# A spectral layer with a routed mixture of experts: first transfers reordered, expert tiles woven in pairs

## The chip, the cores and the metric

The kernel runs on one core of one Trainium2 chip. The metric is device time in microseconds, from the first to the last instruction of one execution; the number quoted for a kernel is the median of several executions. One further execution was taken with the hardware profiler, and all rows below are from it.

## What is computed

```python
X = np.fft.rfft(x, axis=1)                  # x is 8 x 2496 x 256, fp32
Yr = Xr @ w_r - Xi @ w_i + b_r              # 256 x 256 weights
Yi = Xr @ w_i + Xi @ w_r + b_i
Yr, Yi = shrink(Yr), shrink(Yi)             # sign(v) * max(|v| - 0.01, 0)
y = np.fft.irfft(Yr + 1j * Yi, n=2496, axis=1)
x = y.reshape(8 * 2496, 256)                # 19968 tokens
logits = x @ w_gate                         # 8 experts
e, g = argmax(logits), softmax(logits)[argmax]
out[token] = g * (max(x @ w1[e], 0) @ w2[e])   # w1 256 x 1024, w2 1024 x 256
```

## The kernel before

**Two stages.** The spectral stage computes the Fourier transforms as products with constant matrices and routes each token to a row of a DRAM table `xs` that is sorted by expert. The expert stage then walks over tiles of 256 rows of `xs`; a tile belongs to one expert.

**The spectral stage.** The length 2496 is split as 39 x 64. `fwd_a` (lines 274 to 287) multiplies pieces of x, loaded by `load_x` (lines 265 to 272, two DMAs per piece), with the constant `far` (or `fer` for the last piece), copies the result from PSUM to `ae` and stores it to a DRAM scratch `spec`. `turn` (lines 289 to 294) loads a transposed part of `spec` as the tile `t1` (`t` in the rows), two DMAs each. `fwd_b` (lines 296 to 304) multiplies it with the constant `bm`; `halves`, `mix` and `shrink` do the complex product with the weights (split into a rounded high part and a remainder, so that each product is three) and the threshold; `inv_b` and `inv_a` transform back with the constants `bi`, `ga` and `iw`. `iw` holds the gate's weights beside an identity, so that routing needs no product of its own. `route` (lines 554 to 629) computes each token's row in `xs` and leaves a list of eleven scatters in `self.rows`.

**Order of the work.** `spectral` (lines 402 to 504) writes the order out by hand for TensorE and SP (SyncE, which issues DMAs), and from line 442 on for ScalarE and VectorE too: 80 iterations, ten for each of eight batches. An iteration takes one pair of frequencies through `mix`, and holds the transforms of the next batch, the inverse of the last one and the loads four iterations ahead. Before the loop stand: `open_forward` (constants, x of batch 0, the weights, biases, and on POOL's queue nine loads of small constants), 18 warm-up matmuls on zeros, the eleven `fwd_a` of batch 0, `split_constants`, the first `turn`s with the rest of `bm` and the whole of `bi` between them, 17 more warm-up matmuls, and the first `fwd_b`. In iteration 3 the program calls `write_blank` (lines 222 to 232), eight DMAs on POOL's queue that write zero rows ahead of each expert's part of `xs`. Nothing ties them to that iteration.

**Marks.** `pace` (lines 550 to 552) lets POOL copy one element of a tile that was just written; scatters are tied behind the last such copy with a dependency on POOL's own order, and `send` issues one. So scatters are spread over the iterations. Marks are only made while there is something in `self.rows`.

**The expert stage.** There are 85 possible tiles. The last three (`RARE`) run only if a count that is known at run time, `live`, asks for them; 82 run with these inputs. The first five (`EARLY`) can start before the last routing is done. `load` (lines 733 to 750) loads a tile's rows: from tile 5 on as four DMAs for `xq` and one for `xr`. `upright` (lines 801 to 825) transposes them on VectorE (TensorE for the first five) and splits them into `xh` and `xl`. `weights` (lines 752 to 769) loads a tile's expert weights into `r1` and `r2`, two DMAs for w2 and eight for w1, skipped by the DMA itself when the expert is the same as the last tile's. `split1` and `split2` (lines 771 to 799) split them into high and low parts, each a ScalarE copy and a VectorE subtraction in four pieces, and then ask for the next tile's weights.

`step` (lines 896 to 898) does one tile: `up` (lines 827 to 854) makes the hidden layer as four PSUM tiles `ph` of two 128-column blocks, twelve matmuls of 256 columns each; ScalarE takes the Relu into `hh`, VectorE the remainder into `hl`. `down` (lines 856 to 894) makes the outputs in two halves of 128 rows: eight matmuls `hh` x [w2 high, w2 low] of 512 columns and eight `hl` x w2 high of 256 columns per half; then ScalarE and VectorE scale by the gate value (`part`, `o`) and POOL scatters 128 rows of the output. `up` of a tile carries `upright` of the next, `down` carries `split2` and `split1` of the next. `experts_rest` (lines 917 to 941) loops over tiles 3 to 81, then reads `live` on every engine and has three conditionals one after the other.

Of the kernel before, what the change touches and what calls it, by code (L numbers as in the profile page):

```python
# [10 lines left out]
F32 = mybir.dt.float32  # L11
F32R = mybir.dt.float32r
# [12 lines left out]
D = 256  # L25
# [73 lines left out]
class Kernel:  # L99
# [80 lines left out]
    def open_forward(self, st):  # L180
        tc, nc, nb = self.tc, self.nc, self.nb
        f = self.f = self.pool(st, "f", 1, side="right")
        self.xp = self.pool(st, "xp", 5, side="right")
# [10 lines left out]
        self.bias = f.tile([128, 2, D], F32, name="bias")  # L194
        self.bias3 = f.tile([128, 2 * D], BF16, name="bias3")
        nc.vector.memset(self.bias3, 0.0)
        self.xg = {}
# [3 lines left out]
        raw = {}  # L201
# [4 lines left out]
        self.raw = raw  # L206
        for h, b in ((0, self.b_r), (1, self.b_i)):
            nc.gpsimd.dma_start(self.bias[:, h, :], b.rearrange("(o n) -> o n", o=1).broadcast_to((128, D)))
        self.nlam = f.tile([128, 1], F32, name="nlam")
        nc.vector.memset(self.nlam, -LAM)  # L210

        nc.gpsimd.dma_start(self.gar, self.c_ga)
        for c in range(2):
            nc.gpsimd.dma_start(self.iw[:, c, c * 128:c * 128 + 8], self.w_gate[c * 128:(c + 1) * 128, :])
        nc.gpsimd.dma_start(self.ids, self.c_ids)
        nc.gpsimd.dma_start(self.score, self.c_score)
        nc.gpsimd.dma_start(self.base, self.c_base)
        nc.gpsimd.dma_start(self.ltri_f, self.c_ltri)
        nc.gpsimd.dma_start(self.tcol, self.c_tcol)
        nc.gpsimd.memset(self.z[:, :, 64:66, :], 0.0)  # L220

    def write_blank(self):
# [4 lines left out]
        for e in range(E):  # L227
            i = nc.gpsimd.dma_start(self.xs[e * self.cap:e * self.cap + TT, :].rearrange("(p h) c -> p h c", h=2),
                                    blank)
            if e:  # L230
                tc.declare_no_dep(i.ins, group="xs", reason="disjoint rows")
            tc.add_to_no_dep_group("xs", i.ins)

    def split_constants(self):
        nc, f, raw = self.nc, self.f, self.raw
        ws = self.w.tile([128, 2, D], F32, tag="r", name="wsum")
        wd = self.w.tile([128, 2, D], F32, tag="r", name="wdif")
        nc.vector.tensor_sub(wd, raw["i"], raw["r"])
        nc.vector.scalar_tensor_tensor(out=ws, in0=raw["i"], scalar=-1.0, in1=raw["r"], op0=ALU.mult, op1=ALU.subtract)
        raw = {"r": raw["r"], "d": wd, "s": ws}  # L240
        for nm in ("s", "d", "r"):
            self.wh[nm] = f.tile([128, 2, D], F32R, name="wh" + nm)
            self.wl[nm] = f.tile([128, 2, D], F32R, name="wl" + nm)
            nc.scalar.copy(self.wh[nm], raw[nm])
            nc.vector.tensor_sub(self.wl[nm], raw[nm], self.wh[nm])
        self.split_bias()
        nc.scalar.copy(self.gh, self.gar)
        nc.vector.tensor_sub(self.gl, self.gar, self.gh)
        for c in range(2):
            nc.vector.tensor_copy(self.iw[:, c, 8 - 8 * c:136 - 8 * c], self.ident)  # L250
        nc.vector.tensor_copy(self.ltri, self.ltri_f)


# [11 lines left out]
    def load_x(self, b, q):  # L265
        n, j = (4, 3) if q < 5 else (2, 2)
        t = self.xp.tile([117, 4, D], F32, tag="x", name="x")
        for lo, hi in ((0, 32), (32, NA)):
            src = bass.AP(self.x.tensor, self.x[b, NB * lo + 4 * q, 0].offset,
                          [[NB * D, hi - lo], [22 * D, j], [1, n * D]])  # L270
            self.nc.sync.dma_start(t[lo * j:hi * j, :n, :].rearrange("p g d -> p (g d)"), src)
        self.xg[b, q] = t

    def fwd_a(self, b, q, g):
# [5 lines left out]
        ae = self.xp.tile([120, 2, D], F32, tag="ae", name="ae", bufs=8)  # L280
# [121 lines left out]
    def spectral(self, fwd):  # L402
# [563 lines left out]
```

## Time and profile before

| what | us |
|---|---|
| median of 3 runs | 1580.95 |
| lowest, highest | 1579.96, 1581.32 |
| the profiled execution's own time | 1581.68 |
| its span (first to last instruction) | 1579.8 |
| mean granted TensorE clock in it | 0.988 |

How the rows are read: times are us from the start of the span, unless marked ns. PE is TensorE's matmuls and PEld its weight loads, DVE is VectorE, ACT ScalarE, POOL GpSimd, and a q behind an engine's name is its issuing queue (SPq issues DMAs). L841 is line 841 of the kernel. `out<-in` names tiles, `xN` is a count, and what stands in brackets is the idle time of the engine just before and what ended it. A busy time of a group of matmuls counts from its first start to its last modelled end; single matmuls overlap, so the distance between starts is the better measure of pace. PEclk is the granted clock, 1.00 for 2.4 GHz and 0.50 for 1.2 GHz.

### The profile page before, as it was taken

Reading aid. Unit: us, or ns where it says so; the run is one execution under the profiler, and the core shown is the slowest. Engines: PE = TensorE matmul, PEld = TensorE weight load, DVE = VectorE, ACT = ScalarE, POOL = GpSimd, SP = SyncE. Lnnn points to the kernel's source line nnn. Section 1 sums busy time; section 2 is a strip of 40 time slices with the busy share of each in tenths; the row PEclk is TensorE's granted clock in tenths of the full one; section 3 lists DMA queues with packets and bytes.
Section 4 is the critical chain, followed back from the end, with each engine's and each line's share of the span. In section 5 each row is a group of like instructions: output and inputs, shape, how many; then the busy total and the mean of one; then the engine's idle time right before and its main releaser. Section 6 shows DMA issues by size and latency. Waiting matters only on the chain. (4 is left out here: it accounts for less than half of the span.)

```text
span 1579.8 us, 35881 instructions
## 1 busy us (share of the span) xinstructions
PE 1524.4 (96%) x10881; PEld 1398.3 (89%) x10883; DVE 1248.8 (79%) x2685; ACT 1078.5 (68%) x2255; POOL 542.1 (34%) x529
## 2 busy tenths in 40 slices
PE   5999999999999898999999999999999999999996
PEld 2789988988989888889999999999999999999996
DVE  3577776778787987878888888888888888888886
ACT  1577776767677667567676767676767677776765
POOL 2000624244251634723333233334343333333333
PEclk8899999999999999999999999999999999999998
DMA  8753645445462314243223224223214123223120
GB/s 262 214 164 92 192 114 165 139 143 165 130 185 81 120 33 137 83 103 98 51 45 98 49 49 98 48 48 98 49 45 100 45 52 92 55 68 75 42 49 20
DMA packets 182931, 153.81 MB, mean 97 GB/s; under 512 B 120378, under 2 KB 154080, under 8 KB 182477
## 3 DMA queue, kind: packets, MB, share of 16 engines
q1 hardware_dynamic: 162829, 107.17, 26.7%
q0 software_dynamic: 19904, 44.29, 8.5%
q8 instruction: 88, 1.44, 0.4%
q14 instruction: 110, 0.90, 0.2%
HBM read 243.33 MB, written 66.37 MB: 196 GB/s over the span
## 5 line engine op out<-in xcount | busy, mean ns | idle before, releaser
L889 POOL DMA_INDIRECT out<-o,row x154 | 303.7, 1972 | 573.7 <-DVE o L887 548.7
L879 PE MATMUL po<-h,hh 128*128 128x512 f32 x1312 | 462.1, 396 | 0.0
L841 PE MATMUL ph<-xh,h 128*128 128x256 f32 x1312 | 372.8, 284 | 4.0 <-DVE hl L847 2.3
L841 PE MATMUL ph<-xh,l 128*128 128x256 f32 x1312 | 372.1, 284 | 0.5 <-DVE l L782 0.3
L841 PE MATMUL ph<-xl,h 128*128 128x256 f32 x1312 | 371.8, 283 | 0.0
L846 ACT ACTIVATE hh<-ph 128x512 fp32r<-128x512 f32 x328 | 196.0, 597 | 241.0 <-PE ph L841 241.0
L847 DVE SCALAR_TENSOR_TENSOR hl<-ph,hh 128x512 fp32r<-128x512 f32 x328 | 226.7, 691 | 141.0 <-ACT hh L846 130.7
L876 PE MATMUL po<-h,hl 128*128 128x256 f32 x1148 | 321.9, 280 | 0.4 <-DVE hl L847 0.4
L879 PEld LDWEIGHTS po<-h,hh 128*128 128x128 f32 x1312 | 241.4, 188 | 44.4 <-issue 0.2
L841 PEld LDWEIGHTS ph<-xh,h 128*128 128x128 f32 x1312 | 251.9, 192 | 5.0 <-DVE hl L847 3.1
L841 PEld LDWEIGHTS ph<-xh,l 128*128 128x128 f32 x1312 | 252.1, 192 | 4.5 <-DVE l L782 1.0
L841 PEld LDWEIGHTS ph<-xl,h 128*128 128x128 f32 x1312 | 252.0, 192 | 0.0
L876 PEld LDWEIGHTS po<-h,hl 128*128 128x128 f32 x1148 | 217.0, 189 | 4.5 <-DVE hl L847 0.7
L782 DVE TENSOR_TENSOR l<-r,h 128x512 fp32r<-128x512 f32 x332 | 207.1, 686 | 4.4 <-ACT h L781 4.4
L797 DVE TENSOR_TENSOR h<-r,h 128x512 fp32r<-128x512 f32 x332 | 207.1, 685 | 1.2 <-ACT h L796 1.1
L620 POOL DMA_INDIRECT xs_dram<-yb,pos x176 | 180.6, 1026 | 75.5 <-issue 38.1
L781 ACT CAST h<-r 128x512 fp32r<-128x512 f32 x332 | 180.6, 618 | 3.0 <-DMA r<-moe_w 3.0
L796 ACT CAST h<-r 128x512 fp32r<-128x512 f32 x332 | 180.5, 618 | 0.8 <-DMA r<-moe_w 0.8
L358 DVE SCALAR_TENSOR_TENSOR y<-v,r 64x256 f32<-64x256 f32 x320 | 133.9, 418 | 6.8 <-ACT r L352 1.6
L315 DVE TENSOR_TENSOR su<-re,pb 128x256 f32<-128x256 f32 x80 | 33.6, 420 | 91.8 <-ACT sh L314 61.9
L302 PE MATMUL pb<-bm,t 128*128 128x128 f32 x640 | 86.3, 279 | 15.3 <-DMA t<-spec_dram 13.2
L552 POOL COPY mark<-v 1x1 f32<-1x1 f32 x52 | 9.4, 180 | 261.3 <-DVE v L344 261.0
(180 smaller groups left out, 2856.9 us busy)
## 6 DMA issues: line engine op xcount, KB each, us to landing
r<-moe_w SPq DMA_DIRECT2D x178, 512.0 KB
r<-moe_w SPq DMA_DIRECT2D x632, 128.0 KB
spec_dram<-ae SPq DMA_DIRECT2D x88, 240.0 KB
t<-spec_dram SPq DMA_DIRECT2D x160, 128.0 KB
xq<-xs_dram SPq DMA_DIRECT2D x312, 64.0 KB
x<-x SPq DMA_DIRECT2D x40, 384.0 KB
x<-x SPq DMA_DIRECT2D x40, 84.0 KB
xs_dram<-yb,pos POOLq DMA_INDIRECT x176, 3.2
```

The lines of the kernel that those rows point to most:

```text
L358: nc.vector.scalar_tensor_tensor(out=y[q * 64:q * 64 + 64, kp, :], in0=u[h, q, :], scalar=LAM, in1=r[h, q, :], op0=ALU.add, op1=ALU.min)
L620: i = nc.gpsimd.indirect_dma_start(out=self.xs[:, :], out_offset=bass.IndirectOffsetOnAxis(ap=pos[:n, g:g + 1], axis=0), in_=y[:n, g, 0:XW ...
L781: nc.scalar.copy(hi[:, c, s], v)
L782: nc.vector.tensor_sub(lo[:, c, s], v, hi[:, c, s])
L796: nc.scalar.copy(hi[:, s, :], v)
L797: nc.vector.tensor_sub(lo[:, s, :], v, hi[:, s, :])
L841: nc.tensor.matmul(p[:, i, :], a[:, c, f * 128:(f + 1) * 128], v[:, c, :], start=m == 0, stop=m == 5)
L846: nc.scalar.activation(hh[:, s, :], p, AF.Relu)
L847: nc.vector.scalar_tensor_tensor(out=hl[:, s, :], in0=p, scalar=0.0, in1=hh[:, s, :], op0=ALU.max, op1=ALU.subtract)
L876: nc.tensor.matmul(p[:, :D], hl[:, f - 1, hs], w2[:, f - 1, 0, :], start=False, stop=False)
L879: nc.tensor.matmul(p, hh[:, f, hs], w2[:, f].rearrange("p a d -> p (a d)"), start=f == 0, stop=f == 7)
L889: i = nc.gpsimd.indirect_dma_start(out=self.out[:, :], out_offset=bass.IndirectOffsetOnAxis(ap=at[h], axis=0), in_=o[:, h, :], in_offset=N ...
```

## The change

What it does, in the order of the program:

- `open_forward`: `fer`, the smaller DMA of each x piece of batch 0 and later the order on SP change: SP issues `far` and the larger x pieces, ScalarE's queue the smaller ones and `fer`. One more buffer for x, eleven instead of eight for `ae`. The biases come as three rows each (six DMAs of 1 KB on POOL's queue, into a tile that VectorE zeroes) instead of two broadcasts to 128 partitions, and are split ahead of the transforms.
- `load_weights`, then blocks 0 to 3 of `bm`, stand on SP behind the stores of `ae`, right ahead of the first `turn`. The rest of `bm` and all of `bi` go in pieces of four blocks (128 x 512 fp32), in front of the loop and in iterations 0 to 6.
- The nine small constants go on SP's queue in iterations 7 and 8 (`load_late`), and what is computed from them follows in iterations 9 and 10 (`late_constants`).
- `write_blank` becomes a generator in `self.rows`, so each of the eight blocks is issued behind a mark, from iteration 3 on.
- 24 instead of 17 warm-up matmuls ahead of the first `fwd_b`.
- Experts: from tile 3 on, `up(3)` runs alone, then `pair(t)` weaves `down` of tile t with `up` of tile t + 1, four parts of four slots, each slot three matmuls of up and two of down. It carries `split2(t + 1)`, `split1(t + 2)` and `upright(t + 2)`. `hh` and `hl` have a second buffer (pool `hb`) for even tiles. Rows are loaded five tiles ahead instead of four. The last `down(81)` runs alone.
- Nothing is prepared any more for a tile that may not run; `live` is read behind the first `pair`, and the three rare tiles become nested conditionals that load and split their own weights.

```diff
 def open_forward(self, st):
...
-        self.xp = self.pool(st, "xp", 5, side="right")
+        self.xp = self.pool(st, "xp", 6, side="right")
...
         nc.sync.dma_start(far, self.c_fa)
-        nc.sync.dma_start(self.fer, self.c_fe)
...
         for q in range(6):
-            self.load_x(0, q)
-        nc.sync.dma_start(self.bm[:, 0:4, :], self.c_bm[:, 0:4, :])
...
+            self.load_x(0, q, nc.scalar)
+            if q == 1:
+                nc.scalar.dma_start(self.fer, self.c_fe)
+                self.load_bias()
...
+    def load_bias(self):
+        self.bias = self.w.tile([128, 2, D], F32, tag="bias", name="bias", bufs=1)
+        self.nc.vector.memset(self.bias, 0.0)
+        for row in (0, 32, 64):
+            for h, b in ((0, self.b_r), (1, self.b_i)):
+                self.nc.gpsimd.dma_start(self.bias[row:row + 1, h, :], b.rearrange("(o n) -> o n", o=1))
...
+    def load_late(self, part):
+        nc = self.nc
+        if part == 0:
+            nc.sync.dma_start(self.gar, self.c_ga)
+            for c in range(2):
+                nc.sync.dma_start(self.iw[:, c, c * 128:c * 128 + 8], self.w_gate[c * 128:(c + 1) * 128, :])
+            nc.sync.dma_start(self.ltri_f, self.c_ltri)
+        else:
+            nc.sync.dma_start(self.ids, self.c_ids)
+            nc.sync.dma_start(self.score, self.c_score)
+            nc.sync.dma_start(self.base, self.c_base)
+            nc.sync.dma_start(self.tcol, self.c_tcol)
...
 def write_blank(self):
...
-            if e:
-                tc.declare_no_dep(i.ins, group="xs", reason="disjoint rows")
-            tc.add_to_no_dep_group("xs", i.ins)
+            self.behind_mark(i, e > 0)
+            yield
...
 def spectral(self, fwd):
...
         self.keep_warm(18)
+        self.split_bias()
         for i in pairs:
             self.fwd_a(0, *i)
+        self.load_weights()
+        self.blocks(self.bm, self.c_bm, 0, 4)
+        self.turn(0, 0)
         self.split_constants()
-        self.turn(0, 0)
         self.turn(0, 1)
-        self.nc.sync.dma_start(self.bm[:, 4:, :], self.c_bm[:, 4:, :])
+        self.blocks(self.bm, self.c_bm, 4, 8)
         self.turn(0, 2)
         if nb > 1:
             self.load_x(1, 0)
-        self.nc.sync.dma_start(self.bi, self.c_bi)
         self.turn(0, 3)
...
-        self.keep_warm(17)
+        self.keep_warm(24)
...
-            if it == 3:
-                self.write_blank()
+            for at, to, src, lo in ((0, self.bm, self.c_bm, 8), (0, self.bi, self.c_bi, 0),
+                                    (1, self.bm, self.c_bm, 12), (2, self.bi, self.c_bi, 4),
+                                    (3, self.bm, self.c_bm, 16), (4, self.bi, self.c_bi, 8),
+                                    (5, self.bi, self.c_bi, 12), (6, self.bi, self.c_bi, 16)):
+                if at == it:
+                    self.blocks(to, src, lo, lo + 4)
+            if it in (7, 8):
+                self.load_late(it - 7)
...
+            if it == 3:
+                self.rows.append(self.write_blank())
...
+    def pair(self, t):
+        nc = self.nc
+        xh, xl = self.xts.pop(t + 1)
+        h1, l1 = self.ws.pop((t + 1, 1))
+        hh, hl = self.hs.pop(t)
+        w2 = self.ws.pop((t, 2))
+        self.room(t + 1)
+        done = self.outputs(t)
+        splits = itertools.chain(self.split2(t + 1), self.split1(t + 2))
+        turn = self.upright(t + 2)
+        for part in range(4):
+            h, hs = part // 2, slice(part // 2 * 128, part // 2 * 128 + 128)
+            if part % 2 == 0:
+                po = self.psb.tile([128, 512], F32, tag="o", name="po")
+            ph = (self.psb if part % 2 else self.psa).tile([128, 2, TT], F32, tag="h", name="ph")
+            for j in range(4):
+                i, c = j // 2, j % 2
+                f = part * 2 + i
+                for m, (a, v) in enumerate(((h1, xh), (l1, xh), (h1, xl))):
+                    nc.tensor.matmul(ph[:, i, :], a[:, c, f * 128:(f + 1) * 128], v[:, c, :],
+                                     start=c == 0 and m == 0, stop=c == 1 and m == 2)
+                f = part % 2 * 4 + j
+                for g in (f - 1, f) if f == 7 else (f - 1,) if f else ():
+                    nc.tensor.matmul(po[:, :D], hl[:, g, hs], w2[:, g, 0, :], start=False, stop=False)
+                nc.tensor.matmul(po, hh[:, f, hs], w2[:, f].rearrange("p a d -> p (a d)"), start=f == 0, stop=f == 7)
+            next(splits, None)
+            next(turn, None)
+            next(splits, None)
+            self.hidden(t + 1, part, ph)
+            if part % 2:
+                done(h, po)
+        for _ in itertools.chain(splits, turn):
+            pass
...
 def experts_rest(self, late):
...
-        for t in range(t0, main):
-            if t + 4 <= main:
-                self.load(t + 4)
-            self.step(t)
-        live = self.nc.values_load(self.tabs[1][0:1, 3, 0:1], min_val=0, max_val=self.nt)
-        nt = self.nt
-        for t in range(main, nt):
-            with self.tc.If(live > t - self.early):
-                if t > main:
-                    self.nt = t
-                    self.weights_now(t)
-                self.nt = t + 1
-                self.up(t)
-                self.down(t)
+        lead = itertools.chain(self.upright(t0 + 1), self.split1(t0 + 1))
+        self.up(t0, lead)
+        for _ in lead:
+            pass
+        for t in range(t0, main - 1):
+            self.load(t + 5)
+            self.pair(t)
+            if t == t0:
+                live = self.nc.values_load(self.tabs[1][0:1, 3, 0:1], min_val=0, max_val=last)
+        self.down(main - 1)
+        self.rare(live, main, last)
+
+    def rare(self, live, t, last):
+        if t == last:
+            return
+        with self.tc.If(live > t - self.early):
+            self.weights_now(t)
+            self.up(t)
+            self.down(t)
+            self.rare(live, t + 1, last)
```

## Rows read from the trace of the kernel before

**Rows 1.** The page's head and one of its groups of instructions (busy, mean).

```profile
span 1579.8 us, 35881 instructions
...
L879 PE MATMUL po<-h,hh 128*128 128x512 f32 x1312 | 462.1, 396 | 0.0
```

**Rows 2.** Busy time of each engine in chosen stretches, with clock and transfers.

```profile
core 0: us, PE busy (x) PEld busy (x) DVE busy (x) ACT busy (x) POOL busy (x), PEclk, DMA share, GB/s
0.00:36.10 36.10, 21.00 (x57) 7.67 (x58) 11.44 (x32) 6.72 (x11) 11.57 (x27) 0.93 0.83 256
50.40:53.40 3.00, 0.22 (x3) 0.05 (x2) 0.81 (x2) 0.00 (x0) 0.00 (x0) 1.00 0.59 150
53.40:60.90 7.50, 7.50 (x39) 6.12 (x40) 2.94 (x7) 4.22 (x9) 0.00 (x0) 0.77 0.88 250
60.90:83.50 22.60, 22.60 (x157) 18.70 (x156) 14.52 (x32) 15.56 (x35) 0.00 (x0) 1.00 0.62 185
687.09:698.48 11.39, 9.25 (x49) 8.56 (x49) 5.46 (x9) 4.33 (x8) 1.59 (x2) 0.70 0.29 63
704.10:1567.46 863.36, 863.36 (x6081) 808.92 (x6079) 733.77 (x1293) 610.33 (x1141) 299.71 (x153) 1.00 0.26 63
```

**Rows 3.** TensorE in order of time, first 37 us (start us, us, instruction).

```profile
1.40 6.75 PE L509 MATMUL pw<-idle 128*128 128x512 bf16 x18 [1.40 <-DVE idle L155]
...
20.93 1.02 PE L278 MATMUL pa<-x,fer 78*120 78x512 f32 x2
...
36.07 2.05 PE L302 MATMUL pb<-bm,t 128*128 128x128 f32 x8 [10.45 <-DMA t<-spec_dram]
```

**Rows 4.** TensorE in order of time, one tile of the steady expert stage.

```profile
1181.22 0.28 PE L841 MATMUL ph<-xh,h 128*128 128x256 f32 x1
...
1182.28 0.28 PE L841 MATMUL ph<-xh,h 128*128 128x256 f32 x1
...
1186.96 0.40 PE L879 MATMUL po<-h,hh 128*128 128x512 f32 x1
...
1190.14 0.40 PE L879 MATMUL po<-h,hh 128*128 128x512 f32 x1
...
1192.58 0.28 PE L841 MATMUL ph<-xh,h 128*128 128x256 f32 x1
```

**Rows 5.** All engines in order of time, the last instructions of the span.

```profile
1567.22 0.40 PE L879 MATMUL po<-h,hh 128*128 128x512 f32 x1
...
1568.55 0.48 DVE L887 SCALAR_TENSOR_TENSOR o<-po,xr,part 128x256 f32<-128x256 f32 x1
1569.80 0.98 POOL L889 DMA_INDIRECT out<-o,row  x1 [0.30 <-DVEq L935]
```

**Rows 6.** DMA issues by line (count, KB of each, us to landing).

```profile
xs_dram<-blank POOLq DMA_DIRECT2D x8, 264.0 KB, 7.6
...
bi<-c_bi SPq DMA_DIRECT2D x1, 1280.0 KB
...
bias<-b_r POOLq DMA_DIRECT2D x1, 128.0 KB
```

**Rows 7.** SP's queue in order of time, first 61 us (start, us, DMA).

```profile
1.62 10.27 SPq L271 DMA_DIRECT2D x<-x  x12
...
16.48 12.37 SPq L287 DMA_DIRECT2D spec_dram<-ae  x11
32.59 2.60 SPq L293 DMA_DIRECT2D t<-spec_dram  x4
```

**Rows 8.** SP's queue in order of time, 663 to 705 us.

```profile
667.35 1.99 SPq L746 DMA_DIRECT2D xq<-xs_dram  x4
...
678.14 7.39 SPq L769 DMA_DIRECT2D r<-moe_w  x10
```

**Rows 9.** ScalarE in order of time, 685 to 700 us.

```profile
689.18 1.66 ACT L781 CAST h<-r 128x512 fp32r<-128x512 f32 x3 [2.26 <-DMA r<-moe_w]
```

**Rows 10.** Waits, 704 to 1560 us (us in total, times, longest).

```profile
DVE hl L847 <- ACT hh L846: 118.8, 226, 0.8
```

More of the change, by code (lines that the diff above doesn't have):

```diff
@@ L270, in load_x @@
                           [[NB * D, hi - lo], [22 * D, j], [1, n * D]])
-            self.nc.sync.dma_start(t[lo * j:hi * j, :n, :].rearrange("p g d -> p (g d)"), src)
+            (other if other and lo else self.nc.sync).dma_start(t[lo * j:hi * j, :n, :].rearrange("p g d -> p (g d)"), src)
         self.xg[b, q] = t
@@ L622, in scatter @@
                     in_=y[:n, g, 0:XW], in_offset=None, bounds_check=E * self.cap - 1, oob_is_err=False)
-                tc.declare_no_dep(i.ins, group="xs", reason="disjoint rows")
-                tc.add_to_no_dep_group("xs", i.ins)
-                tc.add_manual_dep(i.ins, self.paced.ins.name, mybir.DependencyInfo(
-                    mybir.DependencyClass.NoSync, mybir.DependencyReason.DATA), reason="a few rows per slot")
+                self.behind_mark(i)
                 yield
@@ L831, in up @@
         h1, l1 = self.ws.pop((t, 1))
[L832 to L833 removed]
+        self.room(t)
         for f2 in range(4):
@@ L868, in down, with done @@
         o = self.w2p.tile([128, 2, D], F32, tag="o", name="o", bufs=2)
+        def done(h, p):
+            part = self.w2p.tile([128, D], F32, tag="part", name="part", bufs=2)
+            nc.scalar.activation(part, p[:, D:], AF.Copy, scale=xr[:, h, 0:1])
+            nc.vector.scalar_tensor_tensor(out=o[:, h, :], in0=p[:, :D], scalar=xr[:, h, 0:1], in1=part,
+                                           op0=ALU.mult, op1=ALU.add)
+            i = nc.gpsimd.indirect_dma_start(
+                out=self.out[:, :], out_offset=bass.IndirectOffsetOnAxis(ap=at[h], axis=0),
+                in_=o[:, h, :], in_offset=None, bounds_check=self.ntok - 1, oob_is_err=False)
+            if t or h:
+                tc.declare_no_dep(i.ins, group="out", reason="every token is in one tile only")
+            tc.add_to_no_dep_group("out", i.ins)
+        return done
+    def down(self, t):
+        nc = self.nc
+        hh, hl = self.hs.pop(t)
+        w2 = self.ws.pop((t, 2))
+        done = self.outputs(t)
         work = (self.split2(t + 1), self.split1(t + 1))
@@ L884, in down @@
                 self.send(2)
-            part = self.w2p.tile([128, D], F32, tag="part", name="part", bufs=2)
-            nc.scalar.activation(part, p[:, D:], AF.Copy, scale=xr[:, h, 0:1])
-            nc.vector.scalar_tensor_tensor(out=o[:, h, :], in0=p[:, :D], scalar=xr[:, h, 0:1], in1=part,
-                                           op0=ALU.mult, op1=ALU.add)
-            i = nc.gpsimd.indirect_dma_start(
-                out=self.out[:, :], out_offset=bass.IndirectOffsetOnAxis(ap=at[h], axis=0),
-                in_=o[:, h, :], in_offset=None, bounds_check=self.ntok - 1, oob_is_err=False)
-            if t or h:
-                tc.declare_no_dep(i.ins, group="out", reason="every token is in one tile only")
-            tc.add_to_no_dep_group("out", i.ins)
+            done(h, p)
     def step(self, t):
@@ L898, in step, with room, hidden @@
         self.down(t)
+    def room(self, t):
+        pool = self.hb if self.hb and t % 2 == 0 else self.w2p
+        self.hs[t] = [pool.tile([128, 8, TT], F32R, tag=n, name=n) for n in ("hh", "hl")]
+    def hidden(self, t, f2, p):
+        nc = self.nc
+        hh, hl = self.hs[t]
+        s = slice(f2 * 2, f2 * 2 + 2)
+        nc.scalar.activation(hh[:, s, :], p, AF.Relu)
+        nc.vector.scalar_tensor_tensor(out=hl[:, s, :], in0=p, scalar=0.0, in1=hh[:, s, :],
+                                       op0=ALU.max, op1=ALU.subtract)
+    def pair(self, t):
+        nc = self.nc
+        xh, xl = self.xts.pop(t + 1)
+        h1, l1 = self.ws.pop((t + 1, 1))
+        hh, hl = self.hs.pop(t)
+        w2 = self.ws.pop((t, 2))
+        self.room(t + 1)
+        done = self.outputs(t)
+        splits = itertools.chain(self.split2(t + 1), self.split1(t + 2))
[23 more added lines that the diff above has]
+            pass
     def experts_begin(self):
```

90 lines of the change are left out of this document (45 added, 45 removed).

## The prediction

> **What bounds the kernel now.** I read the span first, then the table by stretches, then the transfers and the engines' order of time inside the stretches that stood out. The span is 1579.8 us [rows 1]. From 704.10 to 1567.46 us TensorE is busy for the whole 863.36 us at a granted clock of 1.00, while VectorE works 733.77 us of it (85%) and ScalarE 610.33 us (71%) [rows 2]. That stretch holds 6081 matmuls; a tile has 80 (48 up, 32 down), so it is 76 tiles of 11.36 us. No engine is waited for by TensorE there, so work saved on VectorE or ScalarE, or a wait taken away, is worth nothing in it. Only a closer spacing of the matmuls would be.
>
> What isn't full is the start. In the first 36.1 us TensorE's real work is the column transforms, done by about 22 us; then it idles 10.45 us for `t<-spec_dram` [rows 3], and that window moves 256 GB/s [rows 2], which says that transfers set its end. Later TensorE is nearly idle from 50.4 to 53.4 us (0.22 us busy), and the next 7.5 us run at a mean clock of 0.77: part of it is at 1.2 GHz instead of 2.4 after that pause [rows 2]. Two more places lose time: tile 5, where up takes 11.39 us instead of 5.74 at a mean clock of 0.70 [rows 2, 4], and the end, where the last matmul starts at 1567.22 us, 12.6 us before the span's end [rows 1, 5].
>
> **The start.** The first inverse-order product needs, in a chain, x, the copies `ae`, their stores, and the loads `t`. Moved away from in front of it are eight zero blocks of 264 KB (2.16 MB), two biases of 128 KB (0.26 MB) that become six rows of 1 KB, and nine loads of small constants (about 0.29 MB by their shapes) [rows 6]: together 2.7 MB. The window moved 36.1 x 256 = 9.24 MB, so 6.5 MB are left; at the same 256 GB/s this takes 25.5 us instead of 36.1, a gain of 10.6 us. The other bound is the chain itself: TensorE can't start before its warm-up ends at 8.15 us; if x is through by 14 us instead of 20.93 [rows 3] (its 2.5 MB at 256 GB/s take 10 us, behind some 3 us of start), a copy (about 1 us), a store's landing (last stores end their issue near 28.85, the loads of `t` go out at 32.59: 3.7 us [rows 7]) and the first load (36.07 - 32.59 = 3.5 us) end at 22.5 us, a gain of 13.6 us. I take 12.
>
> Putting x on two queues is worth the issue alone: SP issues twelve pieces in 10.27 us, until 11.89 [rows 7], but x keeps coming until 20.93 [rows 3], so transfers, not the issue, set it. I cost it at nothing by itself; ScalarE's seven issues at some 0.86 us each (10.27 / 12) end near 8 us, before the first transform gives it a copy to do. The weights behind the stores take about 0.5 MB out of x's way and still land before the first mix; their splits (ScalarE and VectorE, 0.6 to 0.7 us each) run while `t` is loaded. Eleven instead of eight `ae` buffers take away a wait of the last three copies on landed stores; this lies inside the 12. `bm` in pieces and `bi` in pieces behind the first iteration leave 0.26 MB each ahead of the loads of `t`, where the rest of `bm` and the whole of `bi` (1.31 MB [rows 6]) stand now: the 2.8 us of idle go, and so does most of the 1.2 GHz stretch after it (0.23 x 7.5 = 1.7 us, since 0.5 would be half): I take 4 us together. What is late next: the blocks, the pieces of `bi` and nine constants now move during iterations 0 to 8, some 4 MB. At 60.9 to 83.5 us the queues were busy 0.62 with 185 GB/s [rows 2], so 0.38 x 22.6 us x 300 GB/s = 2.6 MB are free in such a stretch and the rest spreads; the loads of `t` are asked for four iterations ahead. POOL did nothing in that stretch (0.00 us), so the eight blocks behind marks block nobody there. I give back 1 us. Start: -15 us; ends -8 (only the later stall and part of the bytes) and -18.
>
> **The expert tiles.** `pair` runs down of tile t and up of tile t+1 woven: three up products of 256 columns, then one 256-column and one 512-column product of down, sixteen times. The count of products and columns is unchanged, so what counts is spacing. In the steady tile the first nine up products take 1181.22 to 1182.28 = 0.118 us each, the other 39 take 0.120, and the pairs of down 3.18 / 9 = 0.353 us up to 1190.14 and 2.44 / 7 = 0.349 behind it [rows 4]. So after a run of 512-column products the next nine are closer by 2 ns, as if TensorE lived for a while on weights loaded ahead. Woven, every fifth product has 512 columns. Nearest row for up: the 0.118 behind a down; for down the mean (5.62 / 16 = 0.351). Per slot 3 x 0.118 + 0.351 = 0.705, per tile 11.28, that is 0.08 to 0.1 us less; times 76: -7 us. Ends: all at the closest spacing (3 x 0.116, a third of 0.349, + 0.349, 11.15) -16 us, all at the widest (3 x 0.120 + 0.353, 11.41) +4 us; a spacing that the trace does not show at all may lie beyond, so I let the far end go to +14.
>
> [...]
>
> VectorE's and ScalarE's work per tile stays. SP loads x five tiles ahead instead of four; the weights of the next expert are asked for behind the same splits. The splits for tile 82, which is not computed (1312 products of each kind are 82 tiles of 16 [rows 1]), lie beside matmuls; their end saves only what stands in the last chain.
>
> **Around tile 5** the change costs something. Its loads wait for the last scatters (667.35), SP then issues loads and ten weight pieces until 685.5 [rows 8], and ScalarE gets the last of the weights at 689.18 [rows 9]. Now up of tile 5 stands ahead of down of tile 4, so half a tile (5.6 us) of work that used to fill this wait comes behind it. Against that, w1's pieces now go out ahead of the two of w2, 2 x 0.74 us sooner (7.39 / 10). 5.6 - 1.5 = 4.1; some of it falls into the 1.2 GHz stretch that today follows the wait, so I take +3 us, ends 0 and +7.
>
> **The end.** Behind the last matmul stand a copy, the product `o` at 1568.55, the read of the tile count and the last scatter at 1569.80, and three conditionals [rows 5]. The count is now read long before and the skipped conditionals are one. Of the 9 us after 1570.78 the landing stays; I take -2 us, ends 0 and -4.
>
> **Sum.** -15 - 7 + 3 - 2 = -21 us. The profiled execution took 1581.68 us in all, 0.73 above the median of the three runs, 1580.95; from the median it comes to 1560 us.
>
> **The rivals.** (A) Order doesn't matter to TensorE: -14 us, 1567. For it: inside up there is no wait whatever; against it: 0.118 and 0.120 for the same products in one tile. (B) The start is held by x and its stores whatever else moves, and only the later stall goes: -4 instead of -15, 1571. For it: the queues were busy 0.83 in the first window; against it: 2.6 MB of that is not x. (C) All products at the closest spacing or below: -31 or more, 1550 down. (D) The other side: VectorE becomes the bound of a pair. It is in order, each `hl` stands behind ScalarE's `hh`, and in the steady stretch it idles 118.8 us for that, 226 times (0.53 us each) [rows 10]. Its work is 733.77 / 76 = 9.65 us a tile; four full waits in each pair would make 9.65 + 4 x 0.53 = 11.8 us, 0.4 above today, +33 us for 76 tiles, and with -14 for the rest 1600 us. It decides the sign from 14 / 76 = 0.18 us a tile on. Against it: the splits and the transposition now stand between the `hl`s and fill these waits, and TensorE needs an `hl` only one pair later.
>
> **How the numbers follow.** Forecast 0.48 (its own range 1551 to 1569), A 0.22, B 0.10, C 0.12, D 0.08. A measurement of this kernel can tell 0.2%, 3.2 us. Faster by more: all but D and the bad ends of A, B and the far end of the spacing: 0.88. Within: 0.05. Slower: 0.07. The range that leaves out D, the far half of C and the bad ends of B: 1543 to 1575.
>
> **What would show it.** The first `pb<-bm,t` between 22 and 26 us instead of 36.07; no stretch near 50 us with TensorE idle; zero blocks between about 45 and 70 us; tile periods below 11.36 with TensorE still without waits; a longer wait near 680 us; the tail behind the last matmul shorter than 12.6 us. I am wrong if the tile period is 11.5 or more, or if `t` still lands after 30 us.

## The result and the profile after

The changed kernel took 1566.88 us (median of 4 runs, 1565.48 to 1568.38), the kernel before 1581.13 in the same job: a ratio of 0.9909, 95% interval 0.9892 to 0.9926. That is 14.2 us less; 21 were forecast, and 1566.88 lies inside the range, close to rival A's 1567. The profiled execution took 1568.38 us in all, with a span of 1566.6, 13.2 less than [rows 1].

The table of the change by stages answers [rows 2] (columns as there).

```profile
0.00:25.79 25.79, 20.94 (x64) 8.21 (x65) 9.78 (x27) 5.74 (x9) 4.65 (x15) 0.99 0.84 255
25.79:46.58 20.79, 18.73 (x105) 16.09 (x106) 11.42 (x25) 10.64 (x25) 0.00 (x0) 0.77 0.82 228
46.58:60.00 13.42, 13.42 (x96) 11.23 (x95) 7.96 (x17) 8.59 (x20) 1.92 (x6) 1.00 0.96 270
...
186.00:192.40 6.40, 3.88 (x26) 2.99 (x24) 3.90 (x14) 3.31 (x11) 0.18 (x1) 1.00 0.02 6
192.40:195.80 3.40, 3.40 (x17) 3.37 (x17) 2.27 (x7) 0.42 (x2) 0.00 (x0) 0.50 0.47 139
...
675.42:691.60 16.18, 15.23 (x81) 13.25 (x82) 11.96 (x21) 9.89 (x20) 2.13 (x2) 0.79 0.48 125
691.60:1558.05 866.45, 866.45 (x6113) 812.09 (x6111) 725.16 (x1292) 595.40 (x1138) 181.85 (x154) 1.00 0.25 63
```

The window up to the first product with `bm` shrank from 36.1 to 25.8 us at the same 255 GB/s: fewer bytes, not a faster transfer. The stretch without TensorE near 50 us is gone (46.58 to 60.00 is full). The long steady stretch is as full as before. Between them TensorE loses time at 186.0 to 192.4, then runs 3.4 us at half clock, and loses some again at tile 5, with a mean clock of 0.79 over 16.18 us (before 0.70 over 11.39).

TensorE in order of time, for [rows 3, 4]: the last transform and the first product with `bm`, one slot of a woven pair, and the first up product of tiles 8 and 80.

```profile
16.77 1.02 PE L304 MATMUL pa<-x,fer 78*120 78x512 f32 x2
...
25.79 2.05 PE L328 MATMUL pb<-bm,t 128*128 128x128 f32 x8 [2.81 <-DMA t<-spec_dram]
...
714.26 0.28 PE L972 MATMUL ph<-xh,h 128*128 128x256 f32 x1
...
1180.12 0.28 PE L972 MATMUL ph<-xh,h 128*128 128x256 f32 x1
1180.24 0.28 PE L972 MATMUL ph<-xh,l 128*128 128x256 f32 x1
1180.36 0.28 PE L972 MATMUL ph<-xl,h 128*128 128x256 f32 x1
1180.48 0.28 PE L976 MATMUL po<-h,hl 128*128 128x256 f32 x1
1180.60 0.39 PE L977 MATMUL po<-h,hh 128*128 128x512 f32 x1
1180.83 0.28 PE L972 MATMUL ph<-xh,h 128*128 128x256 f32 x1
...
1530.02 0.28 PE L972 MATMUL ph<-xh,h 128*128 128x256 f32 x1
```

Inside the slot every 256-column product is 0.12 us behind the one before, the 512-column one holds 0.23. Over 72 tiles, (1530.02 - 714.26) / 72 = 11.33 us a tile against 11.36.

The end, for [rows 5]: 8.6 us from the last matmul to the end of the span (1566.6), 12.6 before.

```profile
1558.05 0.39 PE L929 MATMUL po<-h,hh 128*128 128x512 f32 x1
...
1559.74 0.97 POOL L905 DMA_INDIRECT out<-o,row  x1 [1.84 <-DVEq L1032]
```

By marks in the two traces (change of each stage, us):

| stage | before | after | change |
|---|---|---|---|
| to the 33rd product with `bm` | 60.92 | 46.58 | -14.3 |
| from there to tile 0 | 562.00 | 565.96 | +4.0 |
| tiles 0 to 2 | 41.01 | 41.82 | +0.8 |
| tile 3 to the last matmul | 903.29 | 903.69 | +0.4 |
| behind the last matmul | 12.58 | 8.55 | -4.0 |

So the start gave nearly what was forecast, and the middle took over a quarter of it back. Up to the last matmul the expert stage gained nothing: the steady tiles win 76 x 0.03 = 2.3 us, and the transition around tile 5 loses 2.7. Its rows, for [rows 8, 9]: SP's queue, ScalarE, TensorE.

```profile
663.00 1.84 SPq L783 DMA_DIRECT2D xq<-xs_dram  x4
...
666.21 1.84 SPq L783 DMA_DIRECT2D xq<-xs_dram  x4
...
670.18 4.70 SPq L806 DMA_DIRECT2D r<-moe_w  x8
...
674.75 0.62 ACT L818 CAST h<-r 128x512 fp32r<-128x512 f32 x1 [7.33 <-DMA r<-moe_w]
...
675.42 0.38 PE L972 MATMUL ph<-xh,h 128*128 128x256 f32 x1 [2.88 <-ACT h L818]
```

The w1 pieces of tile 5 go out behind the rows of tiles 6 and 7, which nobody needs yet. TensorE pauses 2.88 us and is then granted 0.50 from 677.1 for 6.8 us.

The 4.0 us of the middle can be followed by the products with `bm`: from the 201st to the 265th the kernel before takes 53.15 us and the changed one 56.63, to the 321st 56.86 and 55.49, from the 577th to the 633rd 56.25 and 57.92. The first of these differences, 3.5 us, is a pause between two iterations that only the changed kernel has. ScalarE, TensorE, and the DMA view of 185.1 to 187.3 us (its GB/s in 40 slices of 55 ns, its queues with packets, MB and share):

```profile
188.13 0.39 ACT L424 COPY yb<-py 117x272 f32<-117x272 f32 x1 [1.87 <-DMA xs_dram<-yb,pos]
...
191.72 0.38 PE L423 MATMUL py<-zh,gh 120*117 120x272 f32 x1 [2.52 <-ACT k L362]
```

```profile
GB/s 173 173 471 116 58 0 0 0 0 0 0 0 0 0 0 0 0 0 0 0 0 0 0 0 0 0 0 0 0 0 58 0 0 0 0 0 0 0 0 0
...
q0 software_dynamic: 32, 0.04, 6.9%
q8 instruction: 1, 0.02, 4.4%
```

ScalarE's first copy into a `yb` waits until the scatter that last read this buffer has landed. The scatter was issued at 183.66, and all but one of its data packets are through by 185.5; the last moves at 186.8, behind one 16 KB packet of program code that started at 185.26 and took 1.55 us. ScalarE stands, `k` behind it is late, TensorE pauses 2.52 us and then gets half the clock for 3.4. The same happens up to 265.66 (2.45 us), there without a fall of the clock. This second pause is no loss against before: the kernel before has it too, with half the clock behind it, so the changed kernel gains 1.4 us there. The last difference, 1.7 us, is no pause but the clock: up to 544.51 before and 532.42 after, both kernels wait 3.6 us for VectorE's `zl`, and only the changed one gets half the clock behind it. The kernel before at the second pause and at this wait, then the changed one at this wait:

```profile
276.21 0.38 PE L397 MATMUL py<-zh,gh 120*117 120x272 f32 x1 [2.30 <-ACT k L336]
276.50:280.00 3.50, 3.50 (x18) 3.26 (x17) 2.11 (x7) 0.90 (x3) 0.00 (x0) 0.51 0.53 145
544.51 0.39 PE L397 MATMUL py<-zl,gh 120*117 120x272 f32 x1 [3.65 <-DVE zl L389]
544.50:547.90 3.40, 3.34 (x26) 3.11 (x26) 3.32 (x8) 2.45 (x8) 0.70 (x2) 1.00 0.01 5
```

```profile
532.42 0.39 PE L423 MATMUL py<-zl,gh 120*117 120x272 f32 x1 [3.63 <-DVE zl L415]
533.80:537.20 3.40, 3.40 (x17) 3.28 (x15) 3.00 (x7) 2.02 (x5) 1.79 (x3) 0.50 0.09 29
```

### The profile page after: what moved, and what is told of

Read it like the earlier page. It is cut to its first block, busy times and chain, and to the rows that moved or that the text cites. A ratio compares the mean times of both kernels' runs of the same rounds, so it can differ in the third digit from the quotient of the medians.

```text
span 1566.6 us, 35590 instructions
## 1 busy us (share of the span) xinstructions
PE 1524.9 (97%) x10890; PEld 1399.3 (89%) x10890; DVE 1234.5 (79%) x2676; ACT 1059.9 (68%) x2246; POOL 421.5 (27%) x534
## 5 line engine op out<-in xcount | busy, mean ns | idle before, releaser
L977 PE MATMUL po<-h,hh 128*128 128x512 f32 x1248 | 493.9, 396 | 0.0
L905 POOL DMA_INDIRECT out<-o,row x154 | 181.6, 1179 | 683.9 <-DVE o L903 339.6
L972 PE MATMUL ph<-xh,l 128*128 128x256 f32 x1248 | 354.1, 284 | 0.7 <-DVE l L819 0.6
L972 PE MATMUL ph<-xh,h 128*128 128x256 f32 x1248 | 350.3, 281 | 3.1 <-ACT h L818 3.1
L972 PE MATMUL ph<-xl,h 128*128 128x256 f32 x1248 | 352.8, 283 | 0.2 <-DVE xl L861 0.2
L972 PEld LDWEIGHTS ph<-xh,l 128*128 128x128 f32 x1248 | 235.0, 188 | 56.7 <-DVE l L819 1.5
L972 PEld LDWEIGHTS ph<-xh,h 128*128 128x128 f32 x1248 | 236.1, 189 | 3.9 <-ACT h L818 3.9
L833 ACT CAST h<-r 128x512 fp32r<-128x512 f32 x328 | 194.0, 619 | 13.7 <-DMA r<-moe_w 13.7
L818 ACT CAST h<-r 128x512 fp32r<-128x512 f32 x328 | 186.5, 619 | 11.2 <-DMA r<-moe_w 11.2
L409 PE MATMUL pz<-iw,z 128*120 128x136 f32 x704 | 97.5, 282 | 0.8 <-ACT z L401 0.7
L401 ACT COPY z<-pv 128x256 f32<-128x256 f32 x160 | 93.4, 702 | 1.5 <-PE pv L398 1.5
```

Of the source, the lines that this page charges most:

```text
L818: nc.scalar.copy(hi[:, c, s], v)
L833: nc.scalar.copy(hi[:, s, :], v)
L905: i = nc.gpsimd.indirect_dma_start(out=self.out[:, :], out_offset=bass.IndirectOffsetOnAxis(ap=at[h], axis=0), in_=o[:, h, :], in_offset=N ...
L972: nc.tensor.matmul(ph[:, i, :], a[:, c, f * 128:(f + 1) * 128], v[:, c, :], start=c == 0 and m == 0, stop=c == 1 and m == 2)
L977: nc.tensor.matmul(po, hh[:, f, hs], w2[:, f].rearrange("p a d -> p (a d)"), start=f == 0, stop=f == 7)
```

## The experiments

Ratios are to the kernel before in the same job; that one's median was 1581.13, 1580.35, 1577.55, 1598.79 and 1605.46 in the five jobs. In the last two the profiles lose 9 to 16 us between the 393rd product with `bm` (near 360 us) and tile 0, in code that no edit touches but for the buffers of `both`, so their totals are read against their own job only.

### The two halves of the change

`start_only`: the start and middle of the change with the expert stage of before (`experts_rest` of before, lines 917 to 941 there).

> The reordered start and middle with the expert stage of before. Theory 1 (the start gives some 14 us, the middle takes back about 4 in pauses and half-clock stretches, so that tile 0 begins 10.4 us earlier, and nothing of it is lost behind): 10 to 14 us below before, 1567 to 1571, by how many pauses the middle has; first pb product at 25.8 us and the 40-product step behind it at 46.6, as in the changed kernel. Rival (the gain is the experts', the start's is held up by later transfers): less than 5 us below before, above 1576.

`experts_only`: the reverse.

> The start and middle of before with the new expert stage. Theory 1 (the woven tiles pay 3.5 us in the transition at tiles 4 and 5, win 0.03 us on each of 76 pairs, 2.3 us, and the end wins 4.0): 2 to 4 us below before, 1577 to 1579. Rival (the weaving itself brings 7 us or more): 7 or more below before, under 1574. Rival (the weaving loses): level with before or above.

Measured: 0.9939 (0.9910 to 0.9969), that is -9.6 us (-14 to -5), and 0.9972 (0.9955 to 0.9989), -4.4 us (-7 to -2). Both lie a little outside what I expected (10 to 14 and 2 to 4). Both gain, the start about twice as much, and together they make the 14. The rivals "under 5 us from the start" and "7 or more from the tiles" fall, but each by a hair: the intervals reach 4.9 and 7.1. In the profile of `start_only` tile 0 begins at 613.64 and there is no pause of over 1 us at tile 5: from tile 3 to the last matmul it needs 900.93 us. In `experts_only` it is 904.29, with the pause and 9.4 us behind the last matmul.

### The weaving alone

```
-        self.up(t0, lead)
...
-            self.pair(t)
+        for t in range(t0, main):
+            if t > t0:
+                self.load(t + 4)
+            self.step(t)
...
-        self.down(main - 1)
```

> The changed kernel with its tiles from 3 on one after the other, up and then down, as before; nested conditionals, the early read of the count and no preparation of tile 82 are kept. Theory 1 (weaving gives 2.3 us in the steady tiles and costs 3.5 in the transition): a period of 11.36 us a tile instead of 11.33, the transition without its half-clock stretch, the end as short as in the changed kernel, in all level with the changed kernel or up to 2 us below it: 1565 to 1567. Rival (weaving is worth the 7 us or more that the prediction gave it): 1571 or more.

Measured: 0.9934 (0.9911 to 0.9958); the changed kernel has 0.9909 (0.9892 to 0.9926). The totals don't tell the two apart, and the interval of `unwoven`, 1566 to 1574 us, reaches the rival's 1571; the tiles do. The first up product of tiles 8 and 80, unwoven:

```profile
717.07 0.28 PE L877 MATMUL ph<-xh,h 128*128 128x256 f32 x1
...
1534.99 0.28 PE L877 MATMUL ph<-xh,h 128*128 128x256 f32 x1
```

817.92 / 72 = 11.36 us a tile. So the weaving is worth 0.03 us a tile, not 0.08. The transition, though, was no better: TensorE paused 2.84 us up to 679.32 and got 6.8 us of half clock, and tile 3 to the last matmul took 904.31 us. That half of my expectation was wrong. Since `start_only` issues the same loads in the same order without a pause, the order of up and down is not what makes the pause. In `start_only` TensorE waits four times for these weights (0.65, 0.34, 0.91 and 0.34 us), in `unwoven` once 2.84 us, and only there the clock falls; what decides between the two stays open.

`same_weights_adjacent` asked whether the stationary block matters (`(h1, xh), (h1, xl), (l1, xh)` in `pair`).

> The changed kernel with the three up products of a slot in another order, so that the two with the same stationary block follow each other. Theory (TensorE's spacing does not depend on which block or product comes before): 11.33 us a tile from tile 8 to 80, within 0.02. Rival (spacing is set by the load of stationary blocks, and a repeated one is cheaper): 11.2 or less, 10 us less in all.

Measured in one run: 11.33 us a tile, as expected; the rival falls.

### The start, undone part by part

Four kernels with one part of the change as before: the zero blocks at once; x on SP alone; the rest of `bm` and all of `bi` in one piece each; `bm`'s first blocks and the two weights ahead of the stores. A fifth put the small constants and the repeated biases back on GpSimd's queue. (The words behind `#` are not in the code.)

```
-                self.rows.append(self.write_blank())
+                for _ in self.write_blank():      # zeros_early, without behind_mark
...
-            (other if other and lo else self.nc.sync).dma_start(
...
+            self.nc.sync.dma_start(               # x_one_queue
...
-        self.blocks(self.bm, self.c_bm, 4, 8)
+        self.blocks(self.bm, self.c_bm, 4, K1)    # matrices_whole, bi alike
...
+        self.blocks(self.bm, self.c_bm, 0, 4)     # weights_ahead, moved up
+        self.load_weights()
         for i in pairs:
             self.fwd_a(0, *i)
```

> The changed kernel with the eight zero blocks (2.16 MB) issued by GpSimd at once, as before, and everything else of the change kept. The mark of each look is the begin of the first product with bm (25.8 us in the changed kernel, 36.1 before) and of the step 40 products later (46.6 and 60.9). Theory (the start is a matter of bytes ahead of the first x, 2.16 MB at 250 to 300 GB/s): first product 7 to 9 us later, 33 to 35 us, the later step at 54 to 56. Rival (the SP queue's issues set the start, the zero blocks move in its gaps): under 2 us later.

> The changed kernel with all twelve transfers of x issued by SP again. Theory (bytes): less than 1 us later at both marks, 25.8 to 26.8 and 46 to 48. Rival (SP's issues, 0.85 us each, are the bound): 3 to 5 us later.

> The changed kernel with the rest of bm (1 MB) and bi (1.25 MB) each in one transfer, where they stood before. Theory: the first product within 1 us of 25.8, and a pause of 2 to 4 us on a t or on bm before the fifth step with a half-clock stretch behind it, so that the later step begins at 50 to 52 instead of 46.6. Rival (the other savings already make room): later step under 48.

> The changed kernel with the first blocks of bm and the two weights (0.77 MB in all) issued ahead of the stores of the first transform, as before. Theory (bytes): first product 2 to 3 us later, 27.8 to 28.8, the later step at 48.5 to 50. Rival (the two queues fill the DMA engines in the prologue only partly, 191 GB/s in the first 10 us, so that there is room): within 1 us at both marks.

> The changed kernel with the nine small constants and the two biases (each repeated for 128 partitions again, 0.13 MB each) issued by GpSimd ahead of the first stores, as before. The zero blocks held the first bm product up by 5.6 us and the weights by 2.5, 8.1 of the 10.3 us that the change gave there. Theory (the sum is whole, the rest is these loads): first product 1.5 to 3 us later, 27.3 to 28.8 us, the step 40 products later at 47.5 to 49.5. Rival (the parts overlap, nothing is left for these): within 0.7 us of 25.8.

Each ran once (0.9963, 0.9917, 0.9918, 0.9949 and 0.9926 of the kernel before), so the marks are read and not the totals. The first product with `bm` in the first, the fourth and the fifth:

```profile
31.43 2.05 PE L330 MATMUL pb<-bm,t 128*128 128x128 f32 x8 [7.42 <-DMA t<-spec_dram]
```

```profile
28.30 1.13 PE L328 MATMUL pb<-bm,t 128*128 128x128 f32 x8 [3.87 <-DMA t<-spec_dram]
```

```profile
14.90 7.03 PE L304 MATMUL pa<-x,far 117*120 117x512 f32 x12 [2.51 <-DMA x<-x]
...
30.43 1.13 PE L328 MATMUL pb<-bm,t 128*128 128x128 f32 x8 [2.47 <-DMA t<-spec_dram]
```

| part undone | first product, us | 33rd product, us |
|---|---|---|
| none | 25.79 | 46.58 |
| zero blocks | 31.43 (+5.6) | 51.05 (+4.5) |
| x on two queues | 25.34 (-0.5) | 44.03 (-2.6) |
| `bm`, `bi` in pieces | 26.16 (+0.4) | 46.06 (-0.5) |
| weights behind the stores | 28.30 (+2.5) | 47.91 (+1.3) |
| small loads late | 30.43 (+4.6) | 50.11 (+3.5) |

In the seven profiled kernels whose start is that of the change the first mark lies between 25.79 and 26.63, the second between 45.3 and 47.6; less than that is not told apart here. So the start is a matter of what stands in x's way: zeros, small loads and, at the first mark, the weights (at the second their 47.91 is hardly outside and below the 48.5 that I expected). It doesn't go by the byte, though: 2.16 MB of zeros cost 5.6 us, less than the 7 to 9 that I expected, 0.77 MB of weights and `bm` 2.5, and 0.54 MB of small loads 4.6, more than the 1.5 to 3 expected. The small loads stand here ahead of the last pieces of x; TensorE waits 2.51 us for one of these in mid-transform and then runs 3.4 us at half clock. The second queue for x brings nothing. The pieces of `bm` and `bi` bring nothing either: with both whole, no pause on a transfer comes between the first product and the 33rd, so what I expected of it was wrong: the stall near 50 us of before went with the other parts. The three prices, 12.7 us, are more than the 10.3 that the first product gained: single undos overlap and don't add.

### The pause at tile 5

`weights_first` moved the rows of tiles 6 and 7 behind the w1 pieces of tile 5, and every later row load behind its pair.

> The changed kernel with the loads of the rows of tiles 6, 7 and 8 behind the weights of the tile that is needed before them. Theory 1 (TensorE's 3.28 us pause at 672.1 and the half-clock stretch of 6.9 us behind it come from the weights of tile 5, issued behind two tiles' row loads): the pause gone or under 1 us, no half-clock stretch there, 5 to 7 us below the changed kernel, 1560 to 1562. Rival (the weights wait for the buffer that is read by the splits, not for the queue): the pause stays, within 1 us of the changed kernel.

Measured: 0.9911 (0.9885 to 0.9938), no gain where I expected 5 to 7 us: the pause moved one tile on, with 6.8 us at half clock behind it. TensorE in order of time there:

```profile
688.00 0.38 PE L972 MATMUL ph<-xh,h 128*128 128x256 f32 x1 [2.47 <-ACT h L818]
```

ScalarE had waited 7.96 us, until 683.40, for the w2 pieces of tile 5, which went out at 679.24, behind two tiles' rows. So `interleaved` puts the rows of one tile, not two, between two weight loads:

```
-        for t in range(self.early or 4, t0 + 5):
+        for t in range(self.early or 4, t0 + 3):
             self.load(t)
...
+        self.load(t0 + 3)
         for t in range(t0, main - 1):
-            self.load(t + 5)
             self.pair(t)
+            self.load(t + 4)
```

> The changed kernel with one tile's row loads between two weight loads: rows of 5, weights 1 of 5, rows of 6, weights 2 of 5, weights 1 of 6, rows of 7 and so on. Putting all row loads behind weights 1 of tile 5 only moved the pause from tile 5 to tile 6 (2.47 us before 688.0), since weights 2 of tile 5 then went out at 679.2 behind two tiles' rows. Theory (the pause is made by what stands between the weight loads on SP's queue): no pause over 1 us between 660 and 700, no half-clock stretch there; from the begin of tile 3 to the last up product 892 to 894.5 us instead of 897.7 in the changed kernel; total about 3 to 5 us below it. Rival (the two expert weights, 2 MB in a row, are bound by the transfer itself): a pause of 2 us or more stays at tile 5 or 6, within 1.5 us of the changed kernel.

`both` adds a third buffer of `yb` (`bufs=3`; `ae` 9 instead of 11, `xq` 2 instead of 5).

> The interleaved loads, and three buffers of yb instead of two (paid with two ae and three xq buffers less), so that ScalarE's first copy into a yb never waits for a scatter. Theory (in the changed kernel ScalarE waits 1.9 and 1.6 us for the scatter of two halves before, at 188 and 262 us, TensorE pauses 2.8 and 2.7 us and then runs 3.4 us at 1.2 GHz): no pause of over 2 us near 188 or 262, no half-clock stretch behind them, the 320th bm product at 286 to 290 us instead of 295.6, 4 to 7 us less in the spectral stage; with the tiles 1556 to 1561 in all. Rival (something else makes the pauses, the scatter only ends last): the pauses stay at 1.5 us or more, under 2 us gained there.

Measured in one job: `interleaved` 0.9900 (0.9867 to 0.9933), `both` 0.9863 (0.9841 to 0.9885). The interval of `both` lies below that of the changed kernel, 0.9892 to 0.9926, but that is from another job, in which the kernel before took 18 us less, and the changed kernel wasn't run in this one. So the totals alone don't show that `both` beats it; the stretches show where it would. Around tile 5 its SP queue and its stretches are these (columns as before; the first row of stretches is that of the pause at 188 us):

```profile
672.66 4.70 SPq L806 DMA_DIRECT2D r<-moe_w  x8
678.17 1.87 SPq L783 DMA_DIRECT2D xq<-xs_dram  x4
...
682.16 6.60 SPq L806 DMA_DIRECT2D r<-moe_w  x10
```

```profile
186.00:192.40 6.40, 5.64 (x42) 4.84 (x41) 5.75 (x20) 3.67 (x11) 0.18 (x1) 1.00 0.27 71
...
675.42:691.60 16.18, 16.18 (x117) 15.17 (x116) 10.85 (x20) 9.21 (x19) 2.14 (x2) 1.00 0.53 147
```

In `both` there is no pause of TensorE from tile 5 on and no half clock, but one of 1.80 us ahead of the first up product of tile 3 (662.32); in `interleaved` there are two, of 1.01 and 1.03 us (up to 673.06 and 682.08), just over the 1 us that I named. From the first up product of tile 5 to the last matmul: 882.6 us in the changed kernel (675.42 to 1558.05), 884.7 in `weights_first`, 878.6 in `interleaved`, 878.3 in `both`; `same_weights_adjacent`, which has the loads of the changed kernel and ran in the same job as the last two, needs 881.3. That is some 3 to 4 us less, as expected. From tile 3 to the last up product `interleaved` needs 893.6 us against 897.7, also as expected.

The pauses of the middle, as waits from 60 to 300 us (us in total, times, longest), changed kernel and `both`:

```profile
PE py L423 <- ACT k L362: 5.7, 3, 2.5
```

```profile
PE py L423 <- ACT k L362: 2.3, 3, 0.8
PE py L423 <- ACT yb L424: 1.8, 1, 1.8
```

With a third buffer no stretch between 34 and 525 us runs at half clock. That alone says little, since `matrices_whole`, with two, has none between 35 and 530 either: its first pause is missing. What the buffer does is seen at the scatters: in `both` the last data packets of the two scatters of 183.63 and 256.37 still come late, 3.04 and 3.28 us behind the issue, and ScalarE's first copy into the next `yb` doesn't wait (behind the first of them):

```profile
185.82 0.76 ACT L424 COPY yb<-py 117x272 f32<-117x272 f32 x2
```

The line is the last copy into one `yb` and the first into the next, with nothing between them.

From the 33rd to the 393rd product with `bm` `both` takes 311.9 us and `interleaved` in the same job 318.0, 6 us more; the changed kernel in its own job takes 313.9, 2 us more. So a gain of 4 to 7 us there is not shown. The mark that I named came at 292.4 us against 295.6, not at 286 to 290: one pause of 1.8 us up to 246.1 stays.

## Why the prediction was right, and where it was off

**The start** was forecast at -16 up to the 33rd product (12 and 4) and gave -14.3 (10.3 and 4.1). Its working holds for the sum of the bytes: 2.7 MB less at 256 GB/s should end the window at 25.5 us, and it ended at 25.79 at 255 GB/s. Part by part it doesn't hold: a megabyte of zeros cost 2.6 us and one of small loads 8.5 when put back, so that the sum came out is in part luck. The 12 that I took, between that and the chain's 22.5 (its terms add up to 22.2), was too much by 1.7: the last transform began at 16.77, not 14, and a store's landing and the first load together cost about what they did (6.8 us against 7.2). The later stall gave the 4 us forecast for it, though for another reason: not because `bm` and `bi` come in pieces.

**The middle** was to lose 1 us and lost 4. The failed step is "what is late next". I looked for free transfer time for the moved loads, and there was enough. Lost were 3.5 us to a scatter that lands 1.5 us later and a `yb` that had no slack, and 1.7 to half the clock behind a pause of 3.6 us that was there before; 1.4 came back at the second pause, which kept its clock. No term of mine stood for any of these.

The row of code loads fits in all fourteen traces. At the two places a 16 KB code packet starts 0.6 to 2.1 us behind the issue of the last scatter in 23 of the 28 cases (1.60 and 1.10 in the changed kernel). The last data packet then comes 2.5 to 3.7 us behind the issue (3.13 and 3.34), and TensorE pauses 1.8 to 2.5 us wherever `yb` has two buffers. In the other five the code packet starts 3.2 to 3.8 us behind, the last data packet comes at 1.7 to 1.9, and no pause is over 1.2 us. The kernel before is of both kinds: 3.78 at the first place, and 0.88 at the second, with its pause up to 276.21; `x_one_queue` and `matrices_whole` have no pause at the first place (3.80 and 3.84). So the place of the code packet shifts with edits made for other reasons, and which kernel pauses is partly luck. That the wait on the scatter makes the pauses is shown by `both`, where the scatters are as late and the two pauses gone. That the code packet delays the scatter fits every case, but no edit moved the packet alone.

**The steady tiles** were forecast at -7 and gave -2.3. The step that failed: "Nearest row for up: the 0.118 behind a down". In the woven slot the three up products take 0.12 each, as the other 39 of [rows 4] do, so a slot is 11.33 / 16 = 0.708 us, not 0.705. Two nanoseconds in the rows of a timeline that rounds to ten were no ground for a term. This is close to rival A, that order doesn't matter: against `unwoven` the weaving is worth 0.03 us a tile, and `same_weights_adjacent` changes nothing.

**The total** meets rival A's 14 us by luck, as terms that cancel: up to tile 0 the kernel gained 10.3 us instead of 15, tiles 0 to 2 lost 0.8 that nobody forecast, the steady tiles gave 2.3, and the end 2 more than forecast.

**Tile 5** was forecast at +3 and cost +2.7 (+3.5 with the half clock in tile 2). The price was right and the cause half: `unwoven`, with down ahead of up as before, has the pause too; the time is made by row loads between the weight loads, and in `interleaved` most of it falls away without giving up the weaving.

**The end** was forecast at -2 and gave -4.0, the far end. The conditionals are worth most of it. GpSimd's queue increments semaphores for each one that is skipped, three times before and once after (number, shortest, median and longest in ns, first and last start in us):

```profile
L935 POOLq INC_SWDGE_SEM  x3: 1225/1242/1271, 1569.9 to 1573.2; - x3
```

```profile
L1032 POOLq INC_SWDGE_SEM  x1: 1122/1122/1122, 1560.8 to 1560.8; - x1
```

From the first start to the third that is 3.3 us of the 4.0; and `start_only`, with three, has 11.5 us behind its last matmul, `unwoven`, with one, 8.6. The early read of the count can't be the reason on GpSimd: there the read still starts behind the last matmul, at 1559.5, while the other engines read at 669.8 to 685.5.

Rival B (the start is held up anyway), C and D (VectorE binds) fall: VectorE's waits for ScalarE in the steady stretch didn't grow to a wait of TensorE; none is left there.

## What to carry to other kernels

When bytes set a start, count what stands ahead of the first needed load, and expect the gain of all parts, not the sum of single ones. A place that has run without waits may have had no slack: before moving work, look for buffers that come free just in time, since a pause of 2 to 4 us was at times followed by 3.4 or 6.8 us at half clock, which cost half of their length. On one issuing queue, what counts is what stands between two late loads; a reorder that only moves the block one load on gains nothing.

## What the runs showed of the hardware

The output scatters on GpSimd became shorter although nothing of theirs was changed: before, on average 1972 ns, woven 1179, unwoven 1935 (154 each). Two of before and one of after, beside VectorE:

```profile
1180.27 2.98 POOL L889 DMA_INDIRECT out<-o,row  x1 [7.09 <-DVE o L887]
1183.56 0.98 POOL L889 DMA_INDIRECT out<-o,row  x1 [0.30 <-issue]
...
1179.91 2.49 DVE L782 TENSOR_TENSOR l<-r,h 128x512 fp32r<-128x512 f32 x4
```

```profile
1186.20 1.16 POOL L905 DMA_INDIRECT out<-o,row  x1 [4.42 <-DVE o L903]
...
1185.84 0.69 DVE L819 TENSOR_TENSOR l<-r,h 128x512 fp32r<-128x512 f32 x1
1186.43 0.69 DVE L861 TENSOR_TENSOR xl<-xf,xh 128x512 fp32r<-128x512 f32 x1
1187.04 0.69 DVE L819 TENSOR_TENSOR l<-r,h 128x512 fp32r<-128x512 f32 x1
```

Before, 76 of the 154 scatters began inside a run of four subtractions with both inputs in SBUF and took about 3 us; the one shown ended 0.85 us behind its run (1183.25 against 1182.40), and the next, behind the run, took 0.98. The Trainium skill ("SBUF — State Buffer", SBUF: two separate sides) says that a VectorE operation with two SBUF inputs and a GpSimd operation that reads SBUF exclude each other on a shared pair of ports. The rows of before agree with that. The woven row doesn't follow from it alone: that scatter ended at 1187.36, while the third of three such subtractions ran. So why the woven scatters are shorter stays open. It gave no time here, since nothing waits for GpSimd.

And with one 16 KB load of program code close behind a scatter's issue, its last data packet came 1.5 us later (3.13 against 1.66 us), TensorE paused 2.5 us, and 1.7 more went by the clock (half of 3.4); the first of these links is read from the packets, not tried.
